# Six batches in place of seven in a delta rule with a mixture layer behind it: rings of 12, raw weights in other rings, joined transposes

## The chip, the cores and the metric

The kernel runs on one core of a Trainium2 chip. The metric is the device time of one execution in microseconds (us). Before the change the median of three runs was 514.68 us (513.51 to 562.13).

## What is computed

For 4 batches and 8 heads a state of 48 x 48 goes through 768 steps of a delta rule. Its outputs, 3072 tokens of 384 values, go through a layer of two products with a softmax gate and a normalisation between them.

```python
batch, n_heads, seq, head_dim = (4, 8, 768, 48)
n_tokens, d_model, d_ff = (3072, 384, 1024)

def _attn_ref(q, k, v, beta):
    k_n = k / (np.linalg.norm(k, axis=-1, keepdims=True) + 1e-06)
    state = np.zeros((B, H, D, D), dtype=np.float32)
    for t in range(S):
        kt, vt, bt = (k_n[:, :, t], v[:, :, t], beta[:, :, t, None])
        y[:, :, t] = np.einsum('bhd,bhde->bhe', q[:, :, t], state)
        v_old = np.einsum('bhde,bhd->bhe', state, kt)
        state = state + bt[:, :, :, None] * np.einsum('bhd,bhe->bhde', kt, vt - v_old)
    return y.astype(np.float32)

def _moe_ref(x, w_in, w_out, g_ln):
    h = x @ w_in
    e = np.exp(h - np.max(h, axis=-1, keepdims=True))
    sm = e / (np.sum(e, axis=-1, keepdims=True) + 1e-09)
    solu = h * sm
    mu = np.mean(solu, axis=-1, keepdims=True)
    var = np.mean((solu - mu) ** 2, axis=-1, keepdims=True)
    ln = (solu - mu) / np.sqrt(var + 1e-06) * g_ln
    return (ln @ w_out).astype(np.float32)
```

w_in and w_out come as 64-bit floats. They are loaded as pairs of 32-bit words, put together by shifts, and split into a high and a low half of 16 bits each.

## The kernel before

**Chunks, units, batches.** The 768 steps are cut into 12 chunks of 64. Two batches and eight heads go side by side on the partitions and in the free dimension, so a chunk is two *units* (`bp` 0 and 1): 24 units, each of 128 tokens for the layer behind. Inside a chunk the steps are tied by a unit lower triangular system of 64 x 64, built from G = K K^T. Its two 32 x 32 diagonal blocks are inverted by columns, for all heads of up to four units at once, with a lane per partition: this is one *batch* m, and it has four units except the first (chunk 0 alone) and the last (chunk 11 alone). So there are NB = 7 batches.

**Stages of a batch.** `load_kq` brings transposed keys and queries (tile kq). `gram` forms G (PSUM tile gram, copied to g and stored to the DRAM tile gd) and the products of queries and keys (qk, masked to pm). `to_inv` reloads G with lanes on the partitions (ginv), `norms` takes the key norms from its diagonal, `inv_begin` scales, `inv_step` does 30 steps of a multiplication (itmp) and an addition (y), `inv_end` stores the inverse and loads it back in the layout of the products (zd to zt, xd to gx and gy). From batch 2 on, POOL does all of a step. In batches 0 and 1, DVE takes the first ten columns and POOL the others. `tlevel` forms the block below the diagonal with small matmuls (mps, msb, zt).

**Stages of a unit.** `chain` needs the batch's zt, the unit's kv, kq and pm and the state st of the unit two before: products kps and yps with the state, r = v - kps, ups, u, then cps (added to st) and the rest of yps. The result goes as a high and a low half (xh, xl) through two DMA transposes (xth, xtl). `moe_h` does 18 matmuls with w_in (h), the maximum, the exponential (e), the product p (pr), its halves ph and pl and their transposes (pth, ptl); `moe_out` does 24 matmuls with w_out (ops) and the store. `column_sums` (cs, csum) needs all of w_out, and every moe_out needs csum.

**Rings.** A tile of a ring waits until an earlier tile's place comes free: kq and pm have 10 places, kv 4, pt and xt 2 for each half, pr 3, e 1. The raw halves of w_out lie in the kq ring, those of w_in in the pr ring; the converted ones in rings of two of their own (wf, wc).

**Order.** Every operation is recorded with an engine, a cost and a priority (`rec.prio`, lower goes first), and `Recorder.order` plans them as a list schedule; each engine then runs its operations in that fixed order. All DMAs are issued by SP. Chains of unit i have priority i - 1, moe_h i + 1.15, moe_out i + 2.5. The conversions of w_in have -8 to -7.5, those of w_out 2.1 to 2.45, and the inversion of batch 1 -10.2 to -10:

```python
    for i in range(8):
        add(load_w_out(i, -1 + 0.05 * i, 2.1 + 0.05 * i))
    for m in range(1, NB):
        f = 4 * m - 2
        e = f if m > 1 else f - 2.5
        tn = e - 5.4 if m > 1 else -10.8
        add(inversion(m, tn + 0.6, e - 2.6 if m > 1 else -10))
    for i, (m, u) in enumerate(order):
        add(chain(m, u, i, i + 0.13, i + 0.25), -CH)
```

Of the kernel before, what the change touches and what calls it, by code (L numbers as in the profile page):

```python
# [7 lines left out]
F16 = mybir.dt.float16  # L8
# [11 lines left out]
NB = 7  # L20
# [267 lines left out]
class Queue:  # L288
# [17 lines left out]
def kernel(  # L306
# [20 lines left out]
    p1, p2, p3, p4, p10 = (pool(f"p{n}", n) for n in (1, 2, 3, 4, 10))  # L327
# [49 lines left out]
    def to_f32(u, raw, scale, n, nm):  # L377
        if raw.dtype == F32:
            dve.tensor_scalar(out=u, in0=raw[:, :n], scalar1=scale, scalar2=None, op0=ALU.mult)
            return  # L380
        w = raw.bitcast(I32)
        lo, hi = w[:, 0 : 2 * n : 2], w[:, 1 : 2 * n : 2]
        c = p2.tile([P, 512], F32, tag="wc", name=f"wc_{nm}")[:, :n]
# [7 lines left out]
        gps.tensor_tensor(out=f, in0=f, in1=c, op=ALU.mult)  # L391

    def load_w_in(k, q, t0, t1):
        yield t0
        f = slice(512 * q, 512 * q + 512)
        raw = p3.tile([P, 512], w_in.dtype, tag="pr", name=f"wi_{k}_{q}")
        sp.dma_start(kb=512, out=raw, in_=w_in[k, q])
        yield t1
        w = p2.tile([P, 512], F32, tag="wf", name=f"wf_{k}_{q}")
        to_f32(w, raw, SC, 512, f"i{k}{q}")  # L400
# [7 lines left out]
    raws = []  # L408

    def load_w_out(k, t0, t1):  # L410
        yield t0
        raw = p10.tile([P, 512], w_out.dtype, tag="kq", name=f"wo_{k}")
        sp.dma_start(kb=384, out=raw[:, :DM], in_=w_out[k])
        raws.append(rec.ops[-1])
        yield t1
        w = p2.tile([P, 512], F32, tag="wf", name=f"wg_{k}")[:, :DM]
        to_f32(w, raw, g_sb[:, k : k + 1], DM, f"o{k}")
        act.copy(out=wout_hi[:, k], in_=w)
        dve.tensor_tensor(out=wout_lo[:, k], in0=w, in1=wout_hi[:, k], op=ALU.subtract)

# [19 lines left out]
    def load_kq(ch, bp):  # L440
        t = p10.tile([P, H, 2, C], F32, tag="kq", name=f"kq_{ch}_{bp}")
        if ch > 4:
            rec.after = raws[-1]
        for b2 in range(2):
            sp.dma_start(kb=192, out=t[dims(b2)], in_=kq[ch, bp, b2])
        rec.after = None
# [11 lines left out]
    def squares(u):  # L458
# [4 lines left out]
        sq = p3.tile([P, H, D], F32, tag="o", name=f"sq_{u}")  # L463
        act.activation(sq, k, AF.Square)
        for v in (u, u + 2):
            dve.tensor_reduce(out=xs[0][:, v], in_=sq, op=ALU.add, axis=AX.X)
# [31 lines left out]
    def gram(m, u, t0):  # L498
# [3 lines left out]
        g = p2.tile([P, H, C], F32, tag="g", name=f"g_{ch}_{bp}")  # L502
        pm = p10.tile([P, H, C], F32, tag="pm", name=f"pm_{ch}_{bp}")
        pt[ch, bp] = pm
        gps_ = ps_f.tile([P, H, C], F32, tag="fl", name=f"gram_{ch}_{bp}")
# [3 lines left out]
        for h2 in range(0, H, 2):  # L509
            with rec.atomic():  # L510
                for h, b2 in hb[2 * h2 : 2 * h2 + 4]:
# [7 lines left out]
                    )  # L519
        rec.after = None  # L520
# [4 lines left out]
        for b2 in range(2):  # L525
            sp.dma_start(kb=128, out=gdt[m][half(b2), u], in_=g[half(1 - b2)])
# [3 lines left out]
    last0 = [None]  # L530

    def to_inv(m):
        gi = p2.tile([P, 32, 32], F32, tag="ginv", name=f"ginv_{m}")
        ginv[m] = gi
        for b in range(4):
            blk = b % 2
            for z in range(1 if len(units(m)) == 4 else 2):
                src = gdt[m].rearrange("t u h j -> t (u h) j")
                n = H * len(units(m))
                ls = slice(0, n)  # L540
# [36 lines left out]
    def inv_end(m):  # L577
# [11 lines left out]
        n = 16 * len(chunks_of(m))  # L589
        src = gdt[m].rearrange("t u h j -> t (u h) j")  # L590
        for b in range(4):
            blk = b % 2
            r0 = 32 * b
            rows = slice(r0, r0 + 32)
            sp.dma_start(kb=128, out=zz[rows, 0:n, blk * 32 : blk * 32 + 32], in_=zd[r0 : r0 + n].rearrange("l j i -> j l i"))
            if blk == 0:
                for t, r1 in ((xx, r0), (xy, r0 + 32)):
                    sp.dma_start(kb=128, out=t[r1 : r1 + 32, 0:n], in_=xd[r0 : r0 + n].rearrange("l j i -> j l i"))
            else:
                sp.dma_start(kb=128, out=xx[rows, 0:n], in_=src[rows, 0:n, 0:32])  # L600
# [48 lines left out]
    def chain(m, u, tb, tu, tk):  # L649
# [59 lines left out]
    def moe_h(ch, bp, t0):  # L709
# [24 lines left out]
        pr = p3.tile([P, DFF], F32, tag="pr", name=f"pr_{nm}")  # L734
# [3 lines left out]
        ph = p1.tile([P, DFF], F16, tag="ph", name=f"ph_{nm}")  # L738
# [190 lines left out]
```

## Time and profile before

| what | value |
|---|---|
| median of three runs | 514.68 us |
| the profiled execution | 512.04 us |
| its span, first to last instruction | 510.2 us |
| mean granted clock of PE | 0.92 |
| busy share of PE, DVE, ACT, POOL | 72, 62, 38, 58% |
| share of the 16 DMA engines, hardware queue | 70.8% |

Engines: PE is the matrix engine, DVE the vector engine, ACT the scalar engine, POOL the general engine, SP the one that issues DMAs (SPq is its queue). Nearly all instructions come from one recording helper, so their line in the profile is the same (L265), and they are told apart by tile: `y<-y,itmp` reads y and itmp and writes y. In a row of the view of groups, "xN | busy, mean ns | idle before" stand behind the shapes. In a timeline row the first two numbers are start and duration in us, and the bracket at the end tells how long the engine had been idle and what ended that. In a row of waits: total, times, longest. In a row of a tile's view: shortest, median and longest duration in ns, then the first and last start in us. In a row of stretches: the stretch and its length, the busy us (and instructions) of PE, PEld, DVE, ACT and POOL, the granted clock, the DMA share and GB/s.

### The profile page before, as it was taken

What the parts mean: (1) busy time and instruction counts of PE and PEld (TensorE: products, weight loads), DVE (VectorE), ACT (ScalarE), POOL (GpSimd) and SP (SyncE); (2) the same over time, 40 slices, a digit from 0 to 9 for tenths busy, and PEclk for the clock granted to TensorE, in tenths of its full rate; (3) what the DMA queues carried; (4) which work ended last, traced back from release to release, by engine and by line L of the source; (5) the groups of instructions that cost most, each with busy time, mean ns of one, the idle gap of its engine ahead of it and who ended that gap; (6) DMA issues with size and microseconds to landing.
All of it is one profiled execution on the core that took longest, in us unless ns stands there. A gap on an engine that the chain in (4) does not pass through costs nothing.

```text
span 510.2 us, 18246 instructions
## 1 busy us (share of the span) xinstructions
PE 368.2 (72%) x7744; PEld 233.9 (46%) x7744; DVE 318.6 (62%) x791; ACT 192.9 (38%) x382; POOL 294.0 (58%) x506
## 2 busy tenths in 40 slices
PE   3510070689579488997598997787969797899974
PEld 3410070455346345665366564444635464566532
DVE  3599999887884383655088664256597355455670
ACT  2210241465522143536144544224345345454450
POOL 3378385966558998984016886008989898100000
PEclk9999999877876699998799998898989899999998
DMA  8685662987989949977999587985656866744332
GB/s 212 159 255 98 155 169 65 161 171 174 172 162 165 179 113 160 168 135 161 189 165 144 145 162 151 160 162 95 107 118 144 145 114 128 131 64 99 73 68 61
DMA packets 180640, 72.21 MB, mean 142 GB/s; under 512 B 165520, under 2 KB 168976, under 8 KB 180560
## 3 DMA queue, kind: packets, MB, share of 16 engines
q1 hardware_dynamic: 180560, 71.06, 70.8%
q8 instruction: 60, 0.98, 0.9%
q14 instruction: 20, 0.16, 0.1%
HBM read 37.21 MB, written 16.52 MB: 105 GB/s over the span
## 4 chain that ended last, share of the span: by engine, by line
POOL 28%; PE 22%; DVE 19%; issue 10%; DMA 9%; SPq 7%; ACT 4%; POOLq 0%; DVEq 0%; ACTq 0%
POOL y L265 13%; POOL itmp L265 11%; PE h L265 7%; SPq L265 7%; PE ops L265 7%; DVE y L265 5%; DVE itmp L265 4%; DMA zt<-zd 3%; DMA ginv<-gd 3%; PE mps L265 2%; DVE wf L265 2%; DVE rst L265 1%; DVE st L265 1%; PE kps L265 1%; PE yps L265 1%
## 5 line engine op out<-in xcount | busy, mean ns | idle before, releaser
L265 POOL TENSOR_TENSOR y<-y,itmp 128x84 f32<-128x84 f32 (+16 forms) x190 | 100.7, 530 | 14.6
L265 POOL TENSOR_TENSOR itmp<-y,ginv 128x84 f32<-128x84 f32 (+16 forms) x190 | 93.3, 491 | 14.0
L265 DVE TENSOR_REDUCE st<-h 128x1 f32<-128x1024 f32 x24 | 29.3, 1222 | 87.5 <-PE h L265 82.2
L265 PE MATMUL qk<-kq 48*64 48x64 f32 x768 | 40.4, 269 | 24.9 <-DVE pm L265 15.6
L265 PE MATMUL gram<-kq 48*64 48x64 f32 x768 | 43.2, 270 | 18.8 <-DMA kq<-kq_dram 11.5
L265 POOL TENSOR_TENSOR st<-st,nhalf 128x1 f32<-128x1 f32 x24 | 13.2, 551 | 64.1 <-DVE st L265 64.1
L265 PEld LDWEIGHTS gram<-kq 48*64 48x64 f32 x768 | 37.5, 178 | 25.7 <-ACT g L265 6.3
L265 PEld LDWEIGHTS <-pth 128*128 128x128 f16 x384 | 37.6, 99 | 25.5 <-issue 1.7
L265 PE MATMUL h<-win_hi,xtl 128*128 128x512 f16 x144 | 45.4, 419 | 5.3 <-DVE pr L265 2.6
L265 PE MATMUL mps<-zt,gx 32*32 32x32 f32 x768 | 13.5, 205 | 48.6 <-issue 28.9
L265 PE MATMUL h<-win_lo,xth 128*128 128x512 f16 x144 | 46.7, 421 | 1.7 <-POOL win_lo L265 1.7
L265 PEld LDWEIGHTS qk<-kq 48*64 48x64 f32 x768 | 35.8, 178 | 25.3 <-DVE pm L265 16.1
L265 PEld LDWEIGHTS <-xth 128*128 128x128 f16 x288 | 28.4, 105 | 39.7 <-issue 14.8
L265 PE MATMUL ops<-wout_hi,ptl 128*128 128x384 f16 x192 | 38.7, 345 | 8.7 <-DMA ptl<-pl 6.8
L265 PE MATMUL h<-win_hi,xth 128*128 128x512 f16 x144 | 43.4, 411 | 0.0
L265 ACT ACTIVATE e<-h,st 128x1024 f32<-128x1024 f32 x24 | 26.7, 1114 | 38.0 <-DVE st L265 26.4
L265 POOL TENSOR_SCALAR_AFFINE_SELECT y<-y 128x1024 f32<-128x1024 f32 x7 | 9.4, 1346 | 53.5 <-DVE y L265 53.5
L265 DVE TENSOR_SCALAR st<-st 128x1 f32<-128x1 f32 (+1 forms) x216 | 35.5, 165 | 5.6
L265 PE MATMUL ops<-wout_lo,pth 128*128 128x384 f16 x192 | 36.9, 334 | 0.0
L265 PEld LDWEIGHTS mps<-zt,gx 32*32 32x32 f32 x768 | 10.1, 117 | 56.9 <-issue 34.8
L265 PE MATMUL ops<-wout_hi,pth 128*128 128x384 f16 x192 | 35.5, 326 | 0.0
L265 PE MATMUL cps<-u,kv 64*64 64x48 f32 x704 | 28.9, 235 | 9.1 <-ACT u L265 3.2
(94 smaller groups left out, 860.4 us busy)
## 6 DMA issues: line engine op xcount, KB each, us to landing
kq<-kq_dram SPq DMA_DIRECT2D x48, 192.0 KB, 4.5
kv<-kv_dram SPq DMA_DIRECT2D x24, 384.0 KB, 4.3
gd<-g SPq DMA_DIRECT2D x48, 128.0 KB, 3.3
out_dram<-oc SPq DMA_DIRECT2D x24, 192.0 KB, 2.2
zd<-y SPq DMA_DIRECT2D x7, 512.0 KB, 2.6
wi<-w_in_dram SPq DMA_DIRECT2D x6, 512.0 KB, 4.4
wo<-w_out_dram SPq DMA_DIRECT2D x8, 384.0 KB, 4.0
ginv<-gd SPq DMA_DIRECT2D x20, 128.0 KB, 4.2
```

Of the source, the lines that this page charges most:

```text
L265: fn(*[real(a) for a in args], **{k: real(a) for k, a in kw.items()})
```

## The change

- Batches hold chunks 2m and 2m + 1, four units each: six batches. Batch 0 now loads four units of keys for its norms, and its order is set anew.
- kq and pm have 12 places. w_out's raw halves go to the kv ring (four places), w_in's to pr (now two places) and, for two of six, to e. The converted weights share the pt ring. Two of batch 0's G use the e ring, and its gram products the PSUM ring of the chains.
- kv loads from chunk 2 on wait for the last raw load of w_out; chunk 0's transposes of p wait for the last conversion.
- The two halves of x and of p lie in one tile and go through one transpose; G is stored in one DMA, without swapping its halves (the loads behind it swap them).
- For batches 0 and 1 the loads of zt, gx and gy go in two halves of lanes.
- Priorities: conversions of w_out at 1.05 to 1.12, chains of batch 0 at i - 14, batch m tied to unit 4m. The planner takes at least 550 ns for a DMA and 1400 ns for a transpose.

```diff
-NB = 7
+NB = NC // 2
-        return self.rec.add(self.name, self.engine.dma_start, (), kw, kb * 5.0, 2000)
+        return self.rec.add(self.name, self.engine.dma_start, (), kw, max(550.0, kb * 5.0), 2000)
-        return self.rec.add(self.name, self.engine.dma_start_transpose, (), kw, kb * 5.0, 2000)
+        return self.rec.add(self.name, self.engine.dma_start_transpose, (), kw, max(1400.0, kb * 5.0), 2500)
 def chunks_of(m):
-    return [ch for ch in (2 * m - 1, 2 * m) if 0 <= ch < NC]
+    return [2 * m, 2 * m + 1]
...
-    def to_f32(u, raw, scale, n, nm):
+    def to_f32(raw, scale, n, nm):
+        w = p2.tile([P, 2, 512], F32, tag="pt", name=f"w_{nm}")
+        u, c = w[:, 0, :n], w[:, 1, :n]
...
-        raw = p10.tile([P, 512], w_out.dtype, tag="kq", name=f"wo_{k}")
-        sp.dma_start(kb=384, out=raw[:, :DM], in_=w_out[k])
+        raw = p4.tile([P, DM], w_out.dtype, tag="kv", name=f"wo_{k}")
+        sp.dma_start(kb=384, out=raw, in_=w_out[k])
...
     def load_kq(ch, bp):
-        t = p10.tile([P, H, 2, C], F32, tag="kq", name=f"kq_{ch}_{bp}")
-        if ch > 4:
-            rec.after = raws[-1]
+        t = p12.tile([P, H, 2, C], F32, tag="kq", name=f"kq_{ch}_{bp}")
...
     def load_kv(ch, bp):
         t = p4.tile([P, H, D + D], F32, tag="kv", name=f"kv_{ch}_{bp}")
+        if ch > 1:
+            rec.after = raws[-1]
         sp.dma_start(kb=384, out=t, in_=kv[ch, bp])
...
-        for b2 in range(2):
-            sp.dma_start(kb=128, out=gdt[m][half(b2), u], in_=g[half(1 - b2)])
+        sp.dma_start(kb=256, out=gdt[m][:, u], in_=g)
...
-            for z in range(1 if len(units(m)) == 4 else 2):
...
-                sp.dma_start(
-                    kb=128, out=gi[32 * b + 16 * z : 32 * b + 16 * z + n],
-                    in_=src[32 * b : 32 * b + 32, ls, blk * 32 : blk * 32 + 32].rearrange("j l i -> l j i"),
-                )
+            sp.dma_start(kb=128, out=gi[r], in_=src[q, :, blk * 32 : blk * 32 + 32].rearrange("j l i -> l j i"))
...
+        for l in (slice(0, 16), slice(16, 32)) if m < 2 else (slice(0, 32),):
...
+        x2 = p1.tile([P, 2, DM], F16, tag="x2", name=f"x2_{nm}")
+        act.activation(x2[:, 1], yf, AF.Copy, scale=SC)
+        dve.scalar_tensor_tensor(out=x2[:, 0], in0=yf, scalar=SC, in1=x2[:, 1], op0=ALU.mult, op1=ALU.subtract)
+        t = p2.tile([P, 6, P], F16, tag="xt", name=f"xt_{nm}")
+        sp.transpose(kb=192, out=t, in_=x2.rearrange("p a f -> p (a f)"))
+        xt[ch, bp] = t[:, 0:3], t[:, 3:6]
...
+        rec.after = lasts[0] if ch == 0 else None
+        t = p2.tile([P, 16, P], F16, tag="pt", name=f"pt_{nm}")
+        sp.transpose(kb=512, out=t, in_=p2_.rearrange("p a f -> p (a f)"))
+        rec.after = None
...
-        add(load_w_in(i // 2, i % 2, -11.5 if i < 2 else -11.0, -8 + 0.1 * i))
+        add(load_w_in(i // 2, i % 2, -13.38 if i < 3 else -12, -8 + 0.1 * i))
...
-        add(load_w_out(i, -1 + 0.05 * i, 2.1 + 0.05 * i))
-    add(once(2.49, column_sums))
+        add(load_w_out(i, -1 + 0.05 * i, 1.05 + 0.01 * i))
+    add(once(1.14, column_sums))
...
-        f = 4 * m - 2
+        f = 4 * m
...
-        tn = e - 5.4 if m > 1 else -10.8
+        tn = f - 5.4 if m > 2 else f - 7 if m > 1 else -10.8
...
-        add(chain(m, u, i, i + 0.13, i + 0.25), -CH)
+        add(chain(m, u, i, i + 0.13, i + 0.25), -CH if m else -14)
```

More of the change, by code (lines that the diff above doesn't have):

```diff
@@ L326 @@
     cp = pool("cp", 1)
-    p1, p2, p3, p4, p10 = (pool(f"p{n}", n) for n in (1, 2, 3, 4, 10))
+    p1, p2, p3, p4, p12 = (pool(f"p{n}", n) for n in (1, 2, 3, 4, 12))
     dr = pool("dr", 2, space=bass.MemoryType.DRAM)
@@ L391, in to_f32 @@
         gps.tensor_tensor(out=f, in0=f, in1=c, op=ALU.mult)
+        return f
     def load_w_in(k, q, t0, t1):
@@ L395, in load_w_in @@
         f = slice(512 * q, 512 * q + 512)
-        raw = p3.tile([P, 512], w_in.dtype, tag="pr", name=f"wi_{k}_{q}")
+        raw = (p1 if (k, q) in ((1, 0), (2, 1)) else p2).tile(
+            [P, 512], w_in.dtype, tag="e" if (k, q) in ((1, 0), (2, 1)) else "pr", name=f"wi_{k}_{q}",
+        )
         sp.dma_start(kb=512, out=raw, in_=w_in[k, q])
         yield t1
-        w = p2.tile([P, 512], F32, tag="wf", name=f"wf_{k}_{q}")
-        to_f32(w, raw, SC, 512, f"i{k}{q}")
+        w = to_f32(raw, SC, 512, f"i{k}{q}")
         act.copy(out=win_hi[:, k, f], in_=w)
@@ L406, in load_g @@
         dve.tensor_scalar(out=g_sb, in0=g_sb, scalar1=SC, scalar2=None, op0=ALU.mult)
-    raws = []
+    raws, lasts = [], [None]
     def load_w_out(k, t0, t1):
         yield t0
-        raw = p10.tile([P, 512], w_out.dtype, tag="kq", name=f"wo_{k}")
-        sp.dma_start(kb=384, out=raw[:, :DM], in_=w_out[k])
+        raw = p4.tile([P, DM], w_out.dtype, tag="kv", name=f"wo_{k}")
+        sp.dma_start(kb=384, out=raw, in_=w_out[k])
         raws.append(rec.ops[-1])
         yield t1
-        w = p2.tile([P, 512], F32, tag="wf", name=f"wg_{k}")[:, :DM]
-        to_f32(w, raw, g_sb[:, k : k + 1], DM, f"o{k}")
+        w = to_f32(raw, g_sb[:, k : k + 1], DM, f"o{k}")
         act.copy(out=wout_hi[:, k], in_=w)
         dve.tensor_tensor(out=wout_lo[:, k], in0=w, in1=wout_hi[:, k], op=ALU.subtract)
+        lasts[0] = rec.ops[-1]
     def rsqrt(out, x, n, nm):
@@ L462, in squares @@
         sp.dma_start(kb=192, out=k, in_=kn[u])
-        sq = p3.tile([P, H, D], F32, tag="o", name=f"sq_{u}")
+        sq = p2.tile([P, H, D], F32, tag="o", name=f"sq_{u}")
         act.activation(sq, k, AF.Square)
-        for v in (u, u + 2):
-            dve.tensor_reduce(out=xs[0][:, v], in_=sq, op=ALU.add, axis=AX.X)
+        dve.tensor_reduce(out=xs[0][:, u], in_=sq, op=ALU.add, axis=AX.X)
     def norms(m):
@@ L519, in gram @@
                     )
+            rec.hold(pm)
         rec.after = None
@@ L588, in inv_end @@
         xy = p1.tile([P, 4 * H, 32], F32, tag="gy", name=f"gy_{m}")
-        n = 16 * len(chunks_of(m))
         src = gdt[m].rearrange("t u h j -> t (u h) j")
[L591 to L600, printed above, removed]
+        for l in (slice(0, 16), slice(16, 32)) if m < 2 else (slice(0, 32),):
+            n = l.stop - l.start
+            for b in range(4):
+                blk = b % 2
+                r0 = 32 * b
+                rows = slice(r0, r0 + 32)
+                lanes = slice(r0 + l.start, r0 + l.stop)
+                sp.dma_start(kb=4 * n, out=zz[rows, l, blk * 32 : blk * 32 + 32], in_=zd[lanes].rearrange("l j i -> j l i"))
+                if blk == 0:
+                    for t, r1 in ((xx, r0), (xy, r0 + 32)):
+                        sp.dma_start(kb=4 * n, out=t[r1 : r1 + 32, l], in_=xd[lanes].rearrange("l j i -> j l i"))
+                else:
+                    sp.dma_start(kb=4 * n, out=xx[rows, l], in_=src[32 * (b ^ 2) : 32 * (b ^ 2) + 32, l, 0:32])
         ztx[m], gxt[m] = zz, (xx, xy)
@@ L844 @@
             add(once(f + u - 0.9, lambda m=m, u=u: fill_v(m, u)))
-        tn = e - 5.4 if m > 1 else -10.8
+        tn = f - 5.4 if m > 2 else f - 7 if m > 1 else -10.8
         add(begin(m, tn, tn + (0.5 if m > 1 else 0.01)))
-        add(inversion(m, tn + 0.6, e - 2.6 if m > 1 else -10))
+        add(inversion(m, tn + 0.6, f - 2.6 if m > 1 else -10))
     order = [(m, u) for m in range(NB) for u in range(len(units(m)))]
@@ L909, in _lay @@
     return {
[L910 removed]
+        "kn_dram": con(kn[:2].reshape(4, P, H, D)),
         "kv_dram": kv,
```

84 lines of the change are left out of this document (38 added, 46 removed).

## The prediction

> **What bounds the kernel now.** I read the page's busy shares and its chain first, to see whether one engine is full.
>
> ```profile
> PE 368.2 (72%) x7744; PEld 233.9 (46%) x7744; DVE 318.6 (62%) x791; ACT 192.9 (38%) x382; POOL 294.0 (58%) x506
> ...
> POOL 28%; PE 22%; DVE 19%; issue 10%; DMA 9%; SPq 7%; ACT 4%; POOLq 0%; DVEq 0%; ACTq 0%
> ```
>
> No engine is full, and the chain goes back and forth between POOL, PE and DVE. So I count in time of PE, the engine with the most to do: span = PE's busy time + PE's idle time. The view of busy time by stretches says where the idle time lies.
>
> ```profile
> core 0: us, PE busy (x) PEld busy (x) DVE busy (x) ACT busy (x) POOL busy (x), PEclk, DMA share, GB/s
> 0.00:100.00 100.00, 30.67 (x839) 26.07 (x840) 79.31 (x195) 22.61 (x41) 61.49 (x113) 0.99 0.68 159
> 100.00:140.00 40.00, 30.31 (x851) 19.05 (x854) 32.41 (x73) 21.71 (x50) 25.95 (x22) 0.76 0.92 172
> 140.00:180.00 40.00, 29.03 (x556) 18.79 (x551) 23.06 (x54) 9.21 (x17) 31.47 (x53) 0.68 0.91 164
> 180.00:210.00 30.00, 26.14 (x490) 16.24 (x489) 19.52 (x46) 13.91 (x27) 26.79 (x50) 1.00 0.78 151
> 210.00:450.00 240.00, 203.13 (x4488) 126.28 (x4486) 133.28 (x343) 100.52 (x204) 144.58 (x261) 0.94 0.75 141
> 450.00:510.00 60.00, 48.96 (x536) 27.51 (x534) 30.99 (x84) 24.94 (x45) 3.70 (x10) 0.97 0.37 74
> ```
>
> Stretch less PE busy gives idle times of 69.3, 9.7, 11.0, 3.9, 36.9 and 11.0 us, 141.8 together; with 368.2 busy that is the span of 510. In the first 100 us DVE is the full engine (79.3), with the first two inversions one behind the other. From 100 to 180 PE is not only idle for 20.7 us: its granted clock is 0.72 on average, so the 59.3 busy us are stretched.
>
> Why is PE short of work from 100 to 180? The timelines of POOL and PE there:
>
> ```profile
> 103.29 1.15 POOL L265 TENSOR_TENSOR win_lo<-wf,win_hi 128x512 f16<-128x512 f32 x1
> ...
> 170.87 0.99 POOL L265 TENSOR_TENSOR wg<-wg,wc_o 128x384 f32<-128x384 f32 x1
> ...
> 179.38 1.54 PE L265 MATMUL ops<-wout_hi,ptl 128*128 128x384 f16 x8 [0.57 <-ACT csum L265]
> ```
>
> The conversion of w_in ends at 104.4, but the last piece of w_out gets through POOL only at 171, between steps of batch 2's inversion. The column sums (csum) need it, and the first output product (ops) waits for them until 179.4. Until then two pt tiles hold the MoE back.
>
> Why is PE short between 210 and 450? Its largest wait there, and the latest inversion start, read backwards:
>
> ```profile
> PE mps L265 <- DMA zt<-zd: 14.0, 4, 5.4
> ```
>
> ```profile
> 298.69 0.42 SPq L265 DMA_DIRECT2D kq<-kq_dram  x1
> ...
> 321.31 1.40 SPq L265 DMA_DIRECT2D gd<-g  x2
> ...
> 344.46 1.26 POOL L265 TENSOR_SCALAR_AFFINE_SELECT y<-y 128x1024 f32<-128x1024 f32 x1 [29.61 <-DVE y L265]
> ```
>
> Four times a batch's first level (mps) waits for the inversion that has just left POOL. That inversion began late because POOL had stood idle for 29.6 us: it needed G, whose last store was issued at 321.3, after keys that came at 298.7, when one of ten places in the kq ring came free.
>
> **The change, part by part.** *One inversion fewer.* The inversions' steps on POOL and their set-up:
>
> ```profile
> L265 POOL TENSOR_TENSOR y<-y,itmp 128x84 f32<-128x84 f32 (+16 forms) x190 | 100.7, 530 | 14.6
> L265 POOL TENSOR_TENSOR itmp<-y,ginv 128x84 f32<-128x84 f32 (+16 forms) x190 | 93.3, 491 | 14.0
> ```
>
> 190 pairs are five batches of 30 and two (shared with DVE) of 20; after it there are 160, and by the means 30 x 1.02 = 31 us of POOL go. PE's matmuls stay the same 24 units, so nothing leaves the 368.2. What the change can take is PE's idle time.
>
> *First 100 us.* SP's queue up to the first inversion, and PE's work beside the second:
>
> ```profile
> 9.23 1.15 SPq L265 DMA_DIRECT2D gd<-g  x2
> ...
> 13.05 1.09 SPq L265 DMA_DIRECT2D gd<-g  x2
> ...
> 16.66 5.22 SPq L265 DMA_DIRECT2D ginv<-gd  x8
> ```
>
> ```profile
> 60.00:88.00 28.00, 10.62 (x322) 9.67 (x322) 25.83 (x67) 6.04 (x18) 21.69 (x45) 1.00 0.51 123
> ```
>
> Batch 0 now holds four units, so two more G before the first inversion, 3.8 us apart if as before (+7.6), against four loads of ginv in place of eight (-2.6) and Gram products that no longer take turns with qk in one PSUM ring (up to 3.8 off again for every second unit). I take +2 (0 to 5). Chains of batch 0 now stand ahead of inversion 1 (priority i - 14 against -10). Before, they stood behind it on DVE:
>
> ```profile
> 87.66 0.18 DVE L265 TENSOR_TENSOR y<-y,itmp 128x10 f32<-128x10 f32 x1
> ...
> 90.14 0.55 DVE L265 COPY st<-cps 128x384 f32<-128x384 f32 x1
> ```
>
> Units 0 and 1 put st and xl, units 2 and 3 also r on DVE, ten instructions at 0.55 us: 5.5 us. Inversion 1 and the conversion of w_in behind it end 2 + 5.5, say 7 us later. In return two levels and two chains come into this stretch, which I estimate at 7 us of PE (10.6 were busy from 60 to 88 with two such units and part of a third's products); an estimated 4 of products with w_in leave it. Idle 69.3 becomes 66. What queues behind a waiting st on DVE is the inversion, so a planner's error shows at once: bounds 58 (nothing late, all of the 10.6 doubled) and 82 (DVE stands some 4 us before each of four chains, the spacing that units had in SP's queue above).
>
> *w_out first.* Its eight conversions move from priority 2.1 to 1.05, ahead of batch 2's inversion:
>
> ```profile
> L265 POOL TENSOR_SCALAR wc_o<-wc_o,g_sb 128x384 f32<-128x384 f32 x8 | 12.9, 1613 | 9.7 <-ACT wc_o L265 9.2
> ...
> L265 POOL TENSOR_TENSOR wg<-wg,wc_o 128x384 f32<-128x384 f32 x8 | 8.3, 1040 | 0.8 <-DVE wg L265 0.5
> ```
>
> 104.4 + 7 + 8 x 2.65 = 132.6 on POOL, plus some 6 us for the last subtraction, the sums and csum: first ops at about 139 in place of 179. Until then PE has h of two units, products of batch 2 and levels of batch 1. Two waits are added on SP: the kv loads of chunk 2 on wait for the last w_out raw, and chunk 0's transposes of p for the last conversion; output stores, kq loads and G stores queue behind them. I keep 12 of the 20.7 us idle (bounds 5 and 30). The clock should rise: 0.76 and 0.68 go with PE shares of 76 and 73%, 0.94 and 1.00 with 85 and 87%. With 12 of 80 idle the share is 85%; at 0.94 the 59.3 us would be 45.4. I take half of that gain, 7 us, since the clock is an average over a toggling one (bounds 0 and 16.6, the last for a clock of 1.00).
>
> The Trainium skill's page "TensorE: Matmul & The Clock Gate" (Part 1) says that the clock has two states, full after about 3.4 us of sustained work and half after an idle window of that length. By that rule alone the 59.3 would run at full clock, an estimate 16.6 us shorter. The trace agrees only in part: the first 100 us show 0.99 with PE 31% busy.
>
> *Rings of 12 and four units per batch.* Keys of a unit now wait for the chain twelve units before, not ten: two units earlier, at 13.8 us a unit (510.2 - 179.4 over 24) 28 us, which is the 29.6 us that POOL stood idle. With 31 us less to do, POOL can stay a batch ahead. I take away the 14.0 us of waits for zt and some 4 of the waits on chains that the inversion held: of 40.8 idle between 180 and 450, 22.8 stay (bounds 10 and 41, nothing gained).
>
> *Joined transposes and stores.* Transposes of p as the trace has them:
>
> ```profile
> L265 SPq DMA_TRANSPOSE pth<-ph x24: 1231/1258/2602, 127.0 to 495.6; - x24
> ```
>
> 48 issues of 1.25 us leave SP, 60 us in all, if a joined one costs what a single one does (bounds 1.26 and 2.5; I take 1.3). It waits for both halves, but PE begins with the low half, which was the later one; so a unit gets its operands at about the same time (its landing is in no row; 0 to 4 us a unit later), and I book 0, hidden behind the products of other units. SP was in the chain with 7% of 510, or 36 us, so there is cover for an error of some us a unit. The halves of the zt loads in the first two batches add some ten issues each, hidden because the first half goes first.
>
> *Tail.* Its 11.0 idle us are the last unit's own latency: kept.
>
> Sum: 368.2 - 7 + 66 + 12 + 22.8 + 11 = 473.0 us of span. The profiled execution took 512.04 for a span of 510.2, so 474.8; the median of 514.68 is 2.6 higher, so **477 us**.
>
> **The rivals.** (a) *The prologue and w_out eat the gain.* DVE stands in its fixed order behind chains that wait for PE: idle 82 and 30 in place of 66 and 12, no clock gain: 477 + 34 + 7 = 518 at worst, 501 with half of the delays. For it: DVE is at 79% there, with little to give. Against it: POOL is at 61%. (b) *PE's clock recovers fully* and the steady idle falls to 15: 477 - 9.6 - 7.8 = 460. (c) *Nothing to gain in the steady part*, because PE's waits there are the latency of chains, not the inversion: idle stays at 40.8, 477 + 18 = 495; with (a)'s half 519, no change that can be told. (d) *Slower:* kv tiles and w_out raws now share a ring of four. With the units numbered 0 to 23, chunk 2 begins with unit 4: its kv, and so chain 4, starts only when the last raws are converted.
>
> ```profile
> 150.70 0.48 ACT L265 COPY u<-ups 128x384 f32<-128x384 f32 x1 [2.92 <-PE ups L265]
> ...
> 469.65 0.48 ACT L265 COPY u<-ups 128x384 f32<-128x384 f32 x1 [2.23 <-PE ups L265]
> ```
>
> These are chains 4 and 23, the fifth and the last of 24 such rows: 319 us for 19 units, and 40 us to the end. If POOL still lets conversions through only at 171, chain 4 starts at about 180 (raw freed, kv landed, kps), and at this pace the end is 180 + 319 + 40 = 539. It decides from a start of chain 4 after 166. Against it: the conversions' priority, 21.2 us of POOL work, and that pace had POOL's late inversions in it.
>
> **How the numbers follow.** Forecast 0.50 (465 to 492), (a) 0.17, (b) 0.12, (c) 0.12, (d) 0.09. A measurement here tells 2%, or 10.3 us, from no change: faster is below 504.4, slower above 525. The forecast, (b), half of (a) and most of (c) are faster: 0.78; the rest of (a) and (c) make 0.12 same; (d) and a little of (a) 0.10 slower. From 452 to 514 some 8 in 10 are held: all but (d), the worst of (a) and the luckiest of (b).
>
> **What would show it.** Right: first ops at 135 to 150; 160 pairs of steps on POOL; the largest PE wait between 200 and 450 no longer zt; POOL's last inversion done more than 80 us before the end; clock over 0.85 from 100 to 180. Wrong: DVE gaps inside inversion 1 that end with PE; POOL steps of batch 2 between conversions; joined transposes of over 2 us on SP; chain 4 after 166.

## The result and the profile after

The changed kernel takes 526.47 us (median of four runs, 525.21 to 527.58) against 514.1 in the same job: a ratio of 1.0255, 95% interval 1.0208 to 1.0302. The forecast was 477. The profiled execution took 525.21 us for a span of 523.5. Here and below a ratio leaves out runs that were slow as a whole (562.13 us of the kernel before, one run each of e3 and e14).

Busy shares and the chain that ended last, from the page of the changed kernel:

```profile
PE 377.8 (72%) x7744; PEld 242.2 (46%) x7744; DVE 304.1 (58%) x771; ACT 192.2 (37%) x382; POOL 257.3 (49%) x445
...
POOL 36%; PE 21%; issue 15%; DVE 12%; DMA 7%; SPq 5%; ACT 2%; POOLq 0%; DVEq 0%; ACTq 0%
```

POOL lost 36.7 us of work, and yet its share of the chain rose from 28 to 36%: the chain to the end goes through POOL more, not less. Where PE's idle time lies is read as before, from the view by stretches:

```profile
0.00:100.00 100.00, 40.95 (x1202) 33.55 (x1202) 63.94 (x147) 26.01 (x56) 55.84 (x90) 1.00 0.71 168
100.00:140.00 40.00, 24.04 (x501) 17.96 (x500) 36.80 (x94) 12.64 (x21) 22.54 (x37) 0.57 0.66 159
140.00:180.00 40.00, 30.68 (x565) 17.63 (x566) 27.69 (x71) 16.53 (x36) 28.48 (x41) 0.87 0.84 185
180.00:210.00 30.00, 22.62 (x517) 14.62 (x509) 14.96 (x39) 14.41 (x27) 23.88 (x44) 0.89 0.49 112
210.00:450.00 240.00, 199.73 (x4195) 124.17 (x4195) 125.95 (x332) 95.80 (x195) 122.85 (x225) 0.89 0.69 134
450.00:523.50 73.50, 59.73 (x786) 34.26 (x784) 34.76 (x91) 26.84 (x49) 3.70 (x10) 0.93 0.35 71
```

Stretch less PE busy gives idle times of 59.1, 16.0, 9.3, 7.4, 40.3 and 13.8 us. Beside the forecast's terms:

| term | forecast | measured |
|---|---|---|
| PE busy (368.2 less 7 for the clock) | 361.2 | 377.8 |
| idle 0 to 100 | 66 | 59.1 |
| idle 100 to 180 | 12 | 25.3 |
| idle 180 to 450 | 22.8 | 47.7 |
| tail | 11 | 13.8 |

The largest miss, 24.9 us, is in the steady part. There the timeline of SP, the copy of G's last tile for batch 5 (its row in the view of the tile), and then DVE's and POOL's timelines show a chain:

```profile
343.71 0.32 SPq L265 DMA_DIRECT2D gd<-g  x1
...
354.03 0.33 SPq L265 DMA_DIRECT2D zd<-y  x1
...
362.80 0.83 SPq L265 DMA_DIRECT2D zt<-zd  x1
363.68 2.07 SPq L265 DMA_DIRECT2D gd<-g  x1
...
372.67 3.30 SPq L265 DMA_DIRECT2D ginv<-gd  x4
```

```profile
L265 ACT COPY g<-gram x2: 585/585/585, 343.1 to 349.6; 128x512 f32<-128x512 f32 x2
```

```profile
379.78 0.19 DVE L265 TENSOR_SCALAR rst<-ginv 128x32 int32<-128x32 int32 x1 [1.22 <-DMA ginv<-gd]
...
385.17 1.23 DVE L265 TENSOR_TENSOR y<-ginv,nb 128x1024 f32<-128x1024 f32 x1
```

```profile
386.47 2.24 POOL L265 TENSOR_SCALAR_AFFINE_SELECT y<-y 128x1024 f32<-128x1024 f32 x1 [15.52 <-DVE y L265]
```

G's last tile was there at 350.2 (349.6 + 0.585). Its store was issued at 363.68, because in SP's fixed order it stands behind batch 4's store and reload of the inverse (zd at 354.03 to zt at 362.80), which wait for batch 4's inversion. Behind the store come the load of ginv, the norms and the set-up, and only then inversion 5. So POOL works on one inversion, then everything up to the next one's first step follows, while POOL has little to do: 32 us from zd to the select. The same happens at both earlier steps (copies of G at 208.34 and 275.50, stores at 219.76 and 291.07): the three stores lie 10.9, 15.0 and 13.5 us behind data that are ready. At the first of them G itself was also late: its copy came 6 us behind zd (202.62).

The kernel before had this only at some steps. SP's timeline there, batch 3's last store of G, its load of ginv, and then batch 2's inverse:

```profile
162.46 1.18 SPq L265 DMA_DIRECT2D gd<-g  x2
165.30 6.28 SPq L265 DMA_DIRECT2D ginv<-gd  x4
...
187.93 0.33 SPq L265 DMA_DIRECT2D zd<-y  x1
```

There the next inversion is prepared before this one is done, and POOL went from one to the other without a gap (its select at 189.43). In the kernel before, two of the four steps between inversions 2 and 6 had this order; in the changed one, none of the three.

The Trainium skill's page "DMA: Bandwidth & Descriptors" (Anatomy of one DMA, written for the path of gpsimd) says that DMA engines wait for no semaphore: a wait is served by the sequencer that issues, before dispatch. SP's rows agree: what stands behind a waiting zd isn't issued, though it was ready 3.8 us before zd was.

### The profile page after: what moved, and what is told of

It reads as the page before. It is cut to its first block, busy times and chain, and to the rows that moved or that the text cites. A ratio compares the mean times of both kernels' runs of the same rounds, so it can differ in the third digit from the quotient of the medians.

```text
span 523.5 us, 18038 instructions
## 1 busy us (share of the span) xinstructions
PE 377.8 (72%) x7744; PEld 242.2 (46%) x7744; DVE 304.1 (58%) x771; ACT 192.2 (37%) x382; POOL 257.3 (49%) x445
## 4 chain that ended last, share of the span: by engine, by line
POOL 36%; PE 21%; issue 15%; DVE 12%; DMA 7%; SPq 5%; ACT 2%; POOLq 0%; DVEq 0%; ACTq 0%
POOL y L265 15%; POOL itmp L265 14%; PE h L265 7%; PE ops L265 6%; SPq L265 5%; PE ups L265 3%; POOL w_i L265 3%; DMA kn<-kn_dram 2%; DVE y L265 2%; POOL kv L265 2%; DVE itmp L265 2%; DMA ginv<-gd 2%; PE mps L265 2%; DMA zt<-zd 2%; POOL st L265 1%
## 5 line engine op out<-in xcount | busy, mean ns | idle before, releaser
L265 PE MATMUL h<-win_hi,xt 128*128 128x512 f16 x288 | 84.3, 413 | 8.6 <-DVE pr L265 8.6
L265 PE MATMUL ops<-wout_hi,pt 128*128 128x384 f16 x384 | 76.9, 345 | 9.4 <-DMA pt<-p 9.4
L265 PEld LDWEIGHTS <-pt 128*128 128x128 f16 x576 | 56.5, 102 | 50.6 <-DMA pt<-p 10.3
L265 DVE TENSOR_REDUCE st<-h 128x1 f32<-128x1024 f32 x24 | 29.3, 1222 | 84.6 <-PE h L265 71.8
L265 PEld LDWEIGHTS <-xt 128*128 128x128 f16 x432 | 41.1, 104 | 58.8 <-issue 22.3
L265 PE MATMUL h<-win_lo,xt 128*128 128x512 f16 x144 | 44.9, 411 | 0.0
L265 DVE SCALAR_TENSOR_TENSOR p<-pr,st,p 128x1024 f16<-128x1024 f32 x24 | 33.0, 1374 | 16.9 <-ACT p L265 16.7
L265 PE MATMUL ups<-r,zt 64*64 64x48 f32 x704 | 29.3, 240 | 17.0 <-DVE r L265 17.0
L265 PE MATMUL yps<-st,kq 48*64 48x48 f32 x704 | 29.8, 242 | 14.0 <-DVE x L265 13.8
L265 PE MATMUL ops<-wout_lo,pt 128*128 128x384 f16 x192 | 38.3, 345 | 0.0
L265 DVE SCALAR_TENSOR_TENSOR pr<-h,e 128x1024 f32<-128x1024 f32 x24 | 29.3, 1221 | 8.6 <-ACT e L265 8.4
```

Of the source, the lines that this page charges most:

```text
L265: fn(*[real(a) for a in args], **{k: real(a) for k, a in kw.items()})
```

## The experiments

Three theories stood against each other. **A**: the time is one chain of inversions with SP's and DVE's work between them, and a tail behind the last one; for e1 it held from the start, and since e1 from 160 us on. **B**: the units' own pace on PE sets the time, and POOL's gaps only follow. **C**: the joined transposes, or the last batch of now four units, make the difference. In e1, e3 to e5, e9 to e11 and e13 only priorities are shifted; a shift rewrites the order on every engine, not on SP alone. All runs, with the start of the last copy of an inverse (`ginv<-y`, shortest to longest duration, first to last start, in the view of the tile):

| kernel | us | ratio to the kernel before | last copy at | span less that |
|---|---|---|---|---|
| before | 514.1 | 1 | 431.4 | 78.8 |
| changed | 526.47 | 1.0255 [1.0208, 1.0302] | 427.4 | 96.1 |
| e1: ginv of batch 1 earlier | 522.88 | 1.0135 [1.0071, 1.0199] | 423.0 | 95.8 |
| e2: batches 3 to 5 by stream | 582.68 | 1.1297 [1.1243, 1.135] | 436.1 | 145.7 |
| e3: norms of kv earlier | 514.62 | 0.9973 [0.9946, 1.0001] | 417.7 | 95.6 |
| e4: chains of batch 0 later | 525.38 | 1.017 [1.0118, 1.0223] | 430.0 | 96.4 |
| e5: batches 3 to 5 by 4, all of it | 520.03 | 1.0082 [1.0054, 1.011] | 391.8 | 124.0 |
| e6: transposes apart | 524.65 | 1.0178 [1.0137, 1.0219] | 426.9 | 95.7 |
| e7: own ring for w_out | 537.34 | 1.0425 [1.0379, 1.0471] | 437.7 | 95.9 |
| e8: rings of 10 | 524.37 | 1.0172 [1.0138, 1.0207] | 425.9 | 96.5 |
| e9: keys and Gram by 4 | 490.63 | 0.9488 [0.9423, 0.9553] | 361.1 | 128.7 |
| e10: keys and Gram by 2 | 495.61 | 0.9587 [0.9528, 0.9646] | 376.8 | 116.7 |
| e11: by 3, and e1 | 492.74 | 0.9509 [0.9431, 0.9588] | 365.7 | 126.2 |
| e12: e9 with rings of 10 | 496.15 | 0.961 [0.9571, 0.9648] | 387.4 | 106.2 |
| e13: the kernel before, by 2 | 506.08 | 0.9791 [0.9722, 0.986] | 408.7 | 91.4 |
| e14: e9 with transposes apart | 506.83 | 0.9839 [0.9771, 0.9907] | 396.4 | 104.7 |

**The prologue (e1, e4).**

```diff
-        add(begin(m, tn, tn + (0.5 if m > 1 else 0.01)))
+        add(begin(m, tn, tn + (0.5 if m > 1 else 0.01)), 0 if m > 1 else -2.57)
```

> The changed kernel with one priority moved: the reload of batch 1's G (ginv), its norms and its set-up go to -13.36 from -10.8, so that SP issues the reload ahead of batch 0's zd and its 20 loads of zt, gx and gy and not behind them. Theory A (the six inversions are one serial chain from the start to the end, with what lies between two of them on SP and DVE, and the time is its sum): inversion 1 ends some 23 us earlier than 120 us, the inversions behind it follow, and the time falls from 526 to 505 to 515. Theory B (the pace of units on PE sets the time, the inversions only follow it): the prologue gets earlier but the time stays at 520 to 528. Theory C (joined transposes and the last batch of four units make the loss): no change, 524 to 528.

```diff
-        add(chain(m, u, i, i + 0.13, i + 0.25), -CH if m else -14)
+        add(chain(m, u, i, i + 0.13, i + 0.25), -CH)
```

> The changed kernel with one part undone: chains of batch 0 at priority i - 1 as before the change, in place of i - 14, so that inversion 1 has DVE ahead of them. The prediction had the chains' ten instructions cost inversion 1 5.5 us. If that was right and the rest of the delay lies in the reload of G: inversion 1 ends 4 to 8 us earlier than 120, time 518 to 526 by theory A, and no less than 522 by theory B, where the first chains and so the first outputs come later instead.

In e1 the copy of inverse 1 came 21 us earlier (98.5), and batch 2's inversion began no earlier (select at 165 against 161.72). The time is 3.6 us below the changed kernel's (1.0135 against 1.0255, and the intervals don't meet): a small gain, not the 11 to 21 us that theory A from the start had given. Chains of batch 0 later (e4) brought that copy to 118.6 from 119.85, 1.2 us and not the 4 to 8 expected, and no gain in time that can be told. So the prologue is late, but the later inversions hardly hang on it.

**Everything of a batch earlier by stream (e2).**

```diff
-            tg = f - 9 + 0.9 * u if m > 1 else -13.35 + 0.01 * u
+            tg = f - 12 + 0.9 * u if m > 1 else -13.35 + 0.01 * u
-        tn = f - 5.4 if m > 2 else f - 7 if m > 1 else -10.8
+        tn = f - 8.4 if m > 2 else f - 7 if m > 1 else -10.8
-        add(inversion(m, tn + 0.6, f - 2.6 if m > 1 else -10))
+        add(inversion(m, tn + 0.6, f - 5.6 if m > 2 else f - 2.6 if m > 1 else -10))
```

> The changed kernel with priorities of batches 3 to 5 moved: load of keys, products for G, reload of G and the inversion's steps go three units earlier (f - 12 in place of f - 9 and so on), nothing else. By the planned order batch 3's four G stores now stand ahead of zd of batch 2 on SP. Theory A: the 32 to 38 us that POOL stands idle between the end of one inversion and the start of the next fall to under 10 for at least one of three gaps, the last inversion ends at 340 to 400 in place of 428, and the time falls to 480 to 505. Theory B: POOL's gaps go, but PE has no more to do than before: 518 to 528. Theory C: 520 to 528.

582.68 us (1.1297 [1.1243, 1.135]). It says nothing of the theories: the inverse of a batch goes over the matrices of the batch two before it ahead of that one's last chain (batch 3's loads of zt at 257 to 264, unit 7's u at 269.1), which so takes other matrices and waits for a later inversion; what this kernel computes is no longer the same.

**One G store (e3).**

```diff
-            add(once(f + u - 0.9, lambda m=m, u=u: fill_v(m, u)))
+            add(once(f + u - 0.9, lambda m=m, u=u: fill_v(m, u)), -6)
```

> The changed kernel with one priority moved: the scaling of v on POOL (fill_v) goes six units earlier, so that it stands between the steps of the next batch's inversion and not behind its end. A part of theory A: the third and fourth chain of a batch wait for r, r for kv, kv for the end of the next inversion (PE waited 4.7, 4.8 and 4.3 us for r there). If that ties the chains to the inversions, the fourth chain of batches 2 and 3 starts 10 us or more earlier and the time falls by 5 to 15 us, to 511 to 521. Theories B and C: at most 3 us, 523 to 528.

12 us less, in the range expected but not by the way expected: the fourth chains of batches 2 and 3 were to come 10 us earlier, and their u came at 285.3 and 354.4 against 284.1 and 357.7. The norms leave POOL earlier, and one step's written order turns round with them. SP's timeline of this run:

```profile
350.33 0.33 SPq L265 DMA_DIRECT2D gd<-g  x1
...
354.94 1.08 SPq L265 DMA_DIRECT2D ginv<-gd  x2
357.58 0.34 SPq L265 DMA_DIRECT2D zd<-y  x1
```

G of batch 5 now goes out at 350.33, ahead of zd, and inversion 5 starts at 372 in place of 386; the end of the last inversion and of the kernel came 10 us earlier with it. Theory A for one step.

**All of them (e5, e9, e10, e11).** First with set-up and inversion moved as well:

```diff
-            add(once(tg - 0.9 if m > 1 else -13.36, lambda ch=ch, bp=bp: load_kq(ch, bp)))
-            add(gram(m, u, tg))
+            lead = -4 if m > 2 else 0
+            add(once(tg - 0.9 if m > 1 else -13.36, lambda ch=ch, bp=bp: load_kq(ch, bp)), lead)
+            add(gram(m, u, tg), lead)
...
-        add(begin(m, tn, tn + (0.5 if m > 1 else 0.01)))
-        add(inversion(m, tn + 0.6, f - 2.6 if m > 1 else -10))
+        add(begin(m, tn, tn + (0.5 if m > 1 else 0.01)), lead)
+        add(inversion(m, tn + 0.6, f - 2.6 if m > 1 else -10), lead)
```

> Edit: for batches 3 to 5 the keys, Gram products, set-up and inversion get priority 4 earlier among what is ready, and the norms of kv (fill_v) 6 earlier as in the run before. By the written order, SP then has G of batches 3 and 4 ahead of batch 2's reload of its inverse, and all of G of batch 5 ahead of batch 4's. Theory A (from 160 us on the time is one chain: inversion, its reload on SP, the next batch's last G store behind it, the ginv load, the norms, the next inversion; then a fixed tail of 95 to 96 us behind the last inversion): the step from one inversion's end to the next, 73 to 78 us now, falls towards PE's own work for four units, some 60 us at the clock of 0.89; with two or three of three steps shorter by 10 to 14 us the last inversion ends at 390 to 410 and the time is 488 to 508 us. Theory B (the chains of the units on PE set the pace, and POOL's gaps only follow them): the same as with the norms alone, 512 to 520 us.

The last inversion came 36 us earlier, the end only 6, so that the 488 to 508 us expected were missed. ACT's timeline tells why:

```profile
251.91 3.77 ACT L265 COPY ginv<-y 128x1024 f32<-128x1024 f32 x2 [1.51 <-POOL y L265]
...
270.62 0.48 ACT L265 COPY u<-ups 128x384 f32<-128x384 f32 x1 [1.52 <-PE ups L265]
```

The inversions of batches 2 and 3, now of one priority, took turns on POOL and ended together, so that unit 8's chain came at 270.6 in place of 227.3. From there the 15 chains to the last took 202 us, 13.5 each, against 16.7 in the changed kernel. And the tail of 96 us is not fixed, as theory A had it: by these rows it grows with the units that are left when the last inversion ends.

So e9 moves only keys, Gram products and the norms of kv (`lead` of -4 on the first two, -6 on `fill_v` as in e3, nothing on `begin` and `inversion`), e10 the same with -2, e11 with -3 and e1's line:

> Edit: as in the run with priority 4 earlier, but only for the keys and Gram products of batches 3 to 5 (and the norms of kv 6 earlier); set-up and inversion keep their own priority, so that batch 3's inversion does not take turns on POOL with batch 2's, as it did there (both ended at 252 to 254 us). By the written order all of G of a batch then stands ahead of the reload of the batch before it. Theory A with the pace of PE as its floor: the last three inversions run one behind the other without waiting for G, the chain of unit 8 stays at about 228 us, and the units behind it follow at PE's own pace, 12 to 14 us each as in the run before from 270 us on: the last chain at 410 to 440 us, time 455 to 490 us. The rival (something else paces the units, such as DVE or SP, and the gain stays what the norms alone gave): 508 to 520 us.

> Edit: the same with priority 2 earlier in place of 4. By the written order all of G and the ginv load of batch 3 stand ahead of batch 2's reload, one of batch 4's four G stores does, and half of batch 5's ginv load stands ahead of batch 4's. Theory A: gains at the steps 2 to 3 and 4 to 5, little at 3 to 4: 470 to 500 us, between the run with 4 and the one with the norms alone. The rival: 508 to 520 us.

> Edit: priority 3 earlier for keys and Gram products, the norms of kv 6 earlier, and batch 1's ginv load ahead of batch 0's reload as in the first run of these (where inversion 1 ended 21 us earlier, but inversion 2 began no earlier). Theory A: what the earlier inversion 1 gives stays 0 to 4 us, since batch 2's start is not held by it: 455 to 490 us and within 6 us of the two runs beside it. Its rival (the first 160 us set the time, all of it): 20 us less than the run with 4.

490.63, 495.61 and 492.74 us: 5.1, 4.1 and 4.9% faster than the kernel before. e9's timelines of SP, POOL and ACT at the step that was shown above, and its stretches:

```profile
295.04 0.95 SPq L265 DMA_DIRECT2D gd<-g  x1
...
299.74 3.45 SPq L265 DMA_DIRECT2D ginv<-gd  x4
...
313.10 0.43 SPq L265 DMA_DIRECT2D zd<-y  x1
```

```profile
317.72 1.26 POOL L265 TENSOR_SCALAR_AFFINE_SELECT y<-y 128x1024 f32<-128x1024 f32 x1 [3.08 <-DVE y L265]
```

```profile
420.27 0.48 ACT L265 COPY u<-ups 128x384 f32<-128x384 f32 x1 [2.23 <-PE ups L265]
432.37 0.48 ACT L265 COPY u<-ups 128x384 f32<-128x384 f32 x1 [1.17 <-PE ups L265]
444.54 0.48 ACT L265 COPY u<-ups 128x384 f32<-128x384 f32 x1 [1.87 <-PE ups L265]
```

```profile
0.00:100.00 100.00, 41.38 (x1202) 33.69 (x1202) 64.33 (x148) 25.72 (x55) 56.88 (x91) 1.00 0.73 168
100.00:140.00 40.00, 23.57 (x500) 17.16 (x499) 34.92 (x91) 12.95 (x22) 20.05 (x35) 0.57 0.72 165
140.00:180.00 40.00, 29.14 (x645) 17.53 (x645) 31.66 (x75) 18.86 (x42) 24.14 (x32) 0.83 0.77 170
180.00:210.00 30.00, 24.92 (x574) 15.62 (x567) 21.00 (x51) 9.57 (x20) 27.18 (x43) 0.89 0.73 141
210.00:450.00 240.00, 222.02 (x4722) 138.21 (x4721) 141.43 (x369) 113.97 (x229) 128.81 (x241) 0.96 0.75 143
450.00:489.80 39.80, 25.82 (x122) 12.82 (x120) 16.07 (x42) 11.49 (x17) 2.22 (x6) 0.87 0.29 65
```

ginv is loaded 13 us before the inversion in front ends, the next select follows 4.6 us behind zd, and the last inversion is done at 363, 127 us before the end. From then on chains follow each other at 12.1 us: B's pace, which sets the time once A's chain is out of the way. Until then they take 15.4 us each (units 4 to 17, 171.5 to 371.8), and the step from inversion 3 to 4 still has 15 us from zd to the select (255.62 to 271.04), so A's chain is shorter and not gone. PE is busy 93% of the stretch from 210 to 450. Unit 8's chain came at 239.0 and not at 228, and e9 and e11 end just past their range of up to 490. That the earlier ginv of batch 1 (e11) adds nothing that can be told agrees with e1; the 20 us of its rival are excluded.

**Rings, transposes and the raw weights, with the order as it came (e6, e7, e8).**

```diff
-        sp.transpose(kb=192, out=t, in_=x2.rearrange("p a f -> p (a f)"))
+        for a in range(2):
+            sp.transpose(kb=96, out=t[:, 3 * a : 3 * a + 3], in_=x2[:, a])
```

(and in the same way for p, eight blocks of `p2_` at a time)

> Edit: the joined transposes of x and p are issued as two each again, each into its half of the joined tile; all else as after the change. Theory C (a joined transpose makes each unit late, since it waits for both halves and lands later): the units' products start some us earlier, the tail behind the last inversion shrinks from 96 us to below 90, time 505 to 518 us. Theory A: nothing but 48 more issues of 1.2 us on SP, 0 to 5 us slower where SP stands in the chain, and up to 12 us faster where the written order changes (it puts batch 4's last G store ahead of batch 3's reload): 514 to 530 us with the tail still 94 to 98 us.

```diff
-        raw = p4.tile([P, DM], w_out.dtype, tag="kv", name=f"wo_{k}")
+        raw = p3.tile([P, DM], w_out.dtype, tag="wo", name=f"wo_{k}")
-    p1, p2, p3, p4, p12 = (pool(f"p{n}", n) for n in (1, 2, 3, 4, 12))
+    p1, p2, p3, p4, p12 = (pool(f"p{n}", n) for n in (1, 2, 3, 4, 11))
```

> Edit: the raw pieces of w_out get a ring of their own of three places in place of the kv ring, and the rings for keys and masked products have 11 places to make room. Theory A with the start of batch 2's inversion (160.6 us) held by the raw pieces that wait in SP's queue for places of the kv ring: this inversion starts 5 to 10 us earlier, and by the written order G of batch 4 stands ahead of batch 3's reload, which shortens that step by some 12 us: 500 to 515 us. Theory A with the start of batch 2's inversion held by the conversions on DVE and POOL instead: it stays at 158 to 163 us, and only the step of batch 3 to 4 shortens: 510 to 520 us. The rival that 12 places are what the change needs: slower than the changed kernel, over 530 us.

```diff
-    p1, p2, p3, p4, p12 = (pool(f"p{n}", n) for n in (1, 2, 3, 4, 12))
+    p1, p2, p3, p4, p12 = (pool(f"p{n}", n) for n in (1, 2, 3, 4, 10))
```

> Edit: the rings for keys and masked products have 10 places again in place of 12, all else as after the change. The prediction's step (two places more bring a batch's keys 28 us earlier): without them each of the late inversions starts later, 15 to 28 us a batch, over 560 us. Theory A (keys are not what comes last; the last G store is late because it stands behind the reload on SP): 522 to 532 us, inversions within 5 us of where they are.

e6 and e8 move the time by 2 us, which is hardly told from nothing, and the tail stays at 96: the first half of theory C, the joined transposes, falls for this order. Its second half no run tried, and the table speaks for it: the last copy comes 4.0 us earlier than in the kernel before and the end 13.3 us later, so the loss against the kernel before stands behind the last inversion, where four units are left in place of two. That the rest gained only those 4 us is what theory A explains. e7 is 11 us slower than the changed kernel. That is what its rival gave (twelve places are what the change needs, over 530), but e8 with ten places excludes it. Inversion 2 began at 168 (select), later and not earlier, and of batch 4's four loads of ginv only one went ahead of the reload (issued at 287.4; the others from 310.2 on, zd at 291.8). Why inversion 2 came later was not settled.

**The same terms with the order turned (e12, e13, e14).** e12 is e9 with 10 in place of 12, e14 is e9 with e6's lines, e13 this edit in the kernel before:

```diff
-            add(once(tg - 0.9 if m > 1 else -11.8, lambda ch=ch, bp=bp: load_kq(ch, bp)))
-            add(gram(m, u, tg))
+            lead = -2 if m > 2 else 0
+            add(once(tg - 0.9 if m > 1 else -11.8, lambda ch=ch, bp=bp: load_kq(ch, bp)), lead)
+            add(gram(m, u, tg), lead)
```

> Edit: the kernel with keys and Gram products 4 earlier (490.6 us), with rings of 10 in place of 12. If twelve places are worth something only once the order lets G go ahead (the forecast's step, hidden until now): keys of batches 4 and 5 come later, the ginv load of batch 4 stands behind batch 3's reload by the written order, and one or two steps fall back by 5 to 15 us each: 496 to 515 us. If two places never matter: 488 to 493 us.

> Edit: in the kernel before the change, keys and Gram products of batches 3 to 6 get priority 2 earlier (by 4, the rings of 10 leave no place for them). If the order was all that there was to gain, and the change itself gives nothing: 485 to 500 us, like the changed kernel with the turned order. If the kernel before already had most of its G ahead of the reloads (two of its steps between inversions had no gap): little to gain, 503 to 518 us, and the change is worth the difference to 490.6.

> Edit: the kernel with keys and Gram products 4 earlier, with the transposes of x and p issued in two again, each into its half. If a joined transpose costs nothing against two (the forecast's step): 488 to 498 us, some of it from the 48 issues more on SP and from another written order. If joining makes the units late: 478 to 486 us.

Now twelve places are worth some 5.5 us (496.15 against 490.63; the intervals of the ratios don't meet), and through SP's order too: with ten, two of batch 4's four loads of ginv stand behind batch 3's reload (284.4), and its select comes at 297.4 against 271.0. The kernel before gains some 2% by the turned order, the changed one 7%; between the two lie 15 us (506.08 to 490.63), which is what the change brings once the order lets it; not quite like for like, since e13 moves by 2 and leaves the norms of kv where they were (against e10, by 2 as well, it is 10 us). e14 is 16 us slower than e9 and outside both of its ranges; this can't be put down to transposes alone, since its written order is another one. SP's timeline there has the load of batch 4's ginv behind batch 3's reload again:

```profile
259.82 0.38 SPq L265 DMA_DIRECT2D zd<-y  x1
...
290.78 2.93 SPq L265 DMA_DIRECT2D ginv<-gd  x4
```

## Why the prediction was wrong

**Rings of 12, the step that failed.** It took POOL's 29.6 us of idle time for lateness of keys, and concluded that two places more and 31 us less work let POOL "stay a batch ahead". e8 tries the step by itself: with ten places again the changed kernel takes 524.37 us in place of 526.47, and its last copy stays at 426 against 427. That 28 us of earlier keys were close to the 29.6 us was chance. The row of G's last store, at 321.31 in the kernel before, asked for another reading. The products for this tile were done on PE at 305.9, 7 us behind the issue of the last keys. ACT copied them at 313.83, behind the copy of the inverse, which waited for POOL; SP then spent the time from 314.40 to 321.31 on batch 4's reload. So the order on ACT and SP put the store 15 us behind the products; the 23 us from store to select are the work that follows, which earlier keys alone don't shorten:

```profile
310.97 1.99 ACT L265 COPY ginv<-y 128x1024 f32<-128x1024 f32 x1 [6.59 <-POOL y L265]
...
313.83 0.57 ACT L265 COPY g<-gram 128x512 f32<-128x512 f32 x1
```

```profile
310.96 0.36 SPq L265 DMA_DIRECT2D zd<-y  x1
...
320.36 0.86 SPq L265 DMA_DIRECT2D zt<-zd  x1
321.31 1.40 SPq L265 DMA_DIRECT2D gd<-g  x2
```

SP's order is written by the planner, and the change rewrote it: I counted work and places, and never asked which of SP's rows would stand behind which. Batches of four units at all steps left every last G store behind a reload. With the stores ahead of it (e9) the idle time from 180 to 450 is 5.1 + 18.0 = 23.1 us, and the forecast for it was 22.8. That the two agree is luck in part: the idle time went by the order, which the forecast didn't have, and the twelve places that it had are worth 5.5 us there (e12).

**What took the place of the zt waits.** PE's waits between 180 and 450 in the changed kernel:

```profile
PE ups L265 <- DVE r L265: 15.6, 6, 4.8
PE yps L265 <- DVE x L265: 8.6, 3, 4.6
PE h L265 <- DVE pr L265: 6.5, 2, 5.9
PE mps L265 <- DMA zt<-zd: 5.6, 2, 3.1
```

zt fell to 5.6, as the sign asked for, and it meant nothing: r comes late because the norms of kv stand behind the inversion on POOL (the inverse's zd at 280.71, the first norm at 280.63). In e3, with the norms earlier, the wait for r falls to 1.9 us, and the fourth chains come no earlier all the same: x (10.9) and zt (7.7) take its place. A late chain shows wherever its last link happens to be.

**w_out first.** First ops at 139, said the sum:

```profile
161.57 1.47 PE L265 MATMUL ops<-wout_hi,pt 128*128 128x384 f16 x8
```

23 us later than that. The conversions began when expected (112.0 on POOL, forecast 104.4 + 7), but took until 152.4, 40 us and not 21: they were counted in POOL's time alone, and DVE, which has four instructions in each, was busy 36.8 of 40 us from 100 to 140 and came to the first of them only at 120.3, behind inversion 1. That alone doesn't explain it: in e1 DVE was free of inversion 1 from 98 on and busy 29.3 of the 40 us, and yet the conversions ran until 146.6 and the first ops came at 157.5. What else stretches them stays open. Idle 25.3 in place of 12; it stays at 27.3 in e9, so this is the second term that is wrong, by 13 to 15 us, and rival (a), which had up to 30 here, came nearer.

**First 100 us.** "7 us later" for inversion 1: its copy came at 119.85 (before: 87.92), 32 us later. SP accounts for 21 of them, by e1: the load of its ginv stands behind the reload of inversion 0. The ten instructions on DVE, booked at 5.5, cost 1.2 by e4. Most of the rest is inversion 0 itself, whose copy came at 61.9 in place of 53.1 (forecast 2 later). SP's rows:

```profile
65.32 0.39 SPq L265 DMA_DIRECT2D zt<-zd  x1
...
74.20 0.49 SPq L265 DMA_DIRECT2D zt<-zd  x1
...
75.26 4.21 SPq L265 DMA_DIRECT2D ginv<-gd  x4
```

By e1 the 21 us cost 3.6 us of the time; idle was 59.1, below the 66 of the sum, with 1202 matmuls in the stretch and 839 before, since batch 0's units fill PE meanwhile.

**Clock and PE busy.** Forecast 361.2, measured 377.8; the granted clock from 100 to 180 was no better (0.57 and 0.87, 0.72 over both as before). In e9, with PE 93% busy, the clock of the steady part is 0.96 against 0.89 with 83%, and PE is busy 366.8 us: 11 of the 16.6 us went away together with PE's waits. The 366.8 stay above the 361.2, so that of the gain of 7 little came. The Trainium skill's page "TensorE: Matmul & The Clock Gate" (Part 1) gives the full clock to sustained work; the steady part agrees (0.96 with 93%), the start does not: 1.00 from 0 to 100 with PE 41% busy, 0.57 from 100 to 140 with 60%.

**Joined transposes at nothing.** Right. Issue on SP from the views of the tiles, and the medians from issue to landing:

```profile
L265 SPq DMA_TRANSPOSE pt<-p x24: 1616/1926/3347, 151.4 to 508.7; - x24
...
L265 SPq DMA_TRANSPOSE xt<-x x24: 1210/1222/2032, 82.0 to 483.9; - x24
```

```profile
xt<-x SPq DMA_TRANSPOSE x24, 3.0
pt<-p SPq DMA_TRANSPOSE x24, 4.6
```

A joined one takes 1.22 and 1.93 us of SP (the sum: 1.3), and lands about as fast as one half did before (medians then: 3.4 and 3.9 us for x, 4.0 and 4.3 for p). In e6, the changed kernel with the transposes apart, a half lands in 2.8 and 3.9 us.

**One inversion fewer.** 160 pairs, 257.3 against 294.0 us on POOL: right. **Tail.** 13.8 for 11; but behind the last inversion there are now four units and not two, 96 us in place of 79, so that an inversion that ended 4 us earlier gave an end 13 us later. The sign "POOL done 80 us before the end" was met and said nothing, since it didn't ask for how many units were left. The sum booked PE's idle time in the tail, which hardly moved, and not the work that waits there.

**Rival (d)** had the right side, not the right reason. Unit 4's chain stands just past its bound of 166:

```profile
167.00 0.48 ACT L265 COPY u<-ups 128x384 f32<-128x384 f32 x1 [3.73 <-PE ups L265]
```

By (d)'s sum this start gives 167 + 319 + 40 = 526 us, the time measured. That is luck: in e9 the chain comes at 171.50 and the kernel takes 490.63 us, so that start doesn't decide.

Summed up against e9's span of 489.8: the forecast of 473 misses by 15.3 (w_out), 5.6 (PE busy), 3.0 (tail), 0.3 (steady part) and -7.4 (start), 16.8 us. The other 33.7 us of the miss (523.5 less 489.8) went with the turned order. By the rows it is SP's, with G ahead of the reloads; but the norms of kv moved as well (e3, where one step turned with them, gave 10 of these), and no run of the changed kernel parts the two.

## What to carry over

Where one engine issues all DMAs in a fixed order, a change in the stages is first read there: for each store that starts the next long step, ask which waiting transfer stands ahead of it. Here the engine with gaps between its long steps wasn't relieved by fewer of them; it was relieved by what let the next one be ready, and the larger ring showed its 5.5 us only behind that. A wait that goes away on PE proves nothing as long as the chain behind it has another link to show. And where work is put together into larger steps, count what is left to do behind the last of them.

## What was not expected

A transpose of twice the size costs SP less than two: for x no more (1.22 us, as for each half before), for p half as much again (1.93 for 1.26). In the same kernel it lands 0.2 us (x) and 0.7 us (p) later than a half (e6). And the granted clock doesn't follow PE's busy share at the start: 1.00 with 41% up to 100 us, 0.53 to 0.59 with 53 to 62% from 100 to 140 in ten of the kernels (the changed one, e3, e5 to e10, e12, e14), but 0.68 with 47% in e4 and 0.88 with 68% in e11. What it follows there isn't shown.
